# The two PSUM banks of a tile's h made neighbours, in an FFT and MoE kernel whose order a planner writes

## The chip, the cores and the metric

One core of a Trainium2 chip (trn2). The time is device microseconds of one execution, from the median of several runs. PE is TensorE (matmuls), PEld its weight loads, DVE is VectorE, ACT ScalarE, POOL GpSimd and SP SyncE, which issues nearly all DMAs.

## What is computed

Eight batches of x (3136 x 256) go through a spectral mix and then through a feed-forward layer with a softmax gate:

```python
X = np.fft.rfft(x, axis=1);  Xr, Xi = X.real, X.imag
Yr = Xr @ w_r - Xi @ w_i + b_r
Yi = Xr @ w_i + Xi @ w_r + b_i
Yr, Yi = (np.sign(Y) * np.maximum(np.abs(Y) - 0.01, 0.0) for Y in (Yr, Yi))
y = np.fft.irfft(Yr + 1j * Yi, n=3136, axis=1)      # 25088 rows of 256 in all
h = y @ w_in                                        # 256 -> 1024
solu = h * softmax(h)
ln = (solu - mean(solu)) / np.sqrt(var(solu) + 1e-6) * g_ln
out = ln @ w_out                                    # 1024 -> 256
```

## The kernel before, in words

**The work.** The front end of a batch makes the forward transform in two steps (`fwd1`, `fwd2`), the mix with the weights (`mix`), the threshold and the first inverse step (`inv1`); `inv2` writes y, split into two f16 halves, into a ring in SBUF (`ring_hi`, `ring_lo`). The back end takes 196 tiles of 128 rows from the ring. For each tile:

- `moe_head` (L1065): 12 matmuls of 512 columns write h (128 x 1024) into a tile of two PSUM banks, six matmuls into the first bank and six into the second. Then DVE takes the row maximum over both banks (the TENSOR_REDUCE `sm<-banks`), ACT makes the exponential from both banks (ACTIVATE `u<-banks,sm,hsb`), and DVE multiplies h by it (SCALAR_TENSOR_TENSOR `u<-banks,sm,u`). All three read both banks, in this order; only the third is the last reader of h.
- `moe_turn` (L1101): u is split in two f16 halves (ACT `lh`, POOL `ll`), each goes through a DMA transpose into `th` and `tl`, and ACT takes the sum of squares (`junk`).
- `moe_tail` (L1120): 16 matmuls with `th` and then 8 with `tl`, all of 256 columns, add up in one bank `po`; ACT scales it out (`o<-banks,r`).

The back end of batch b runs among the front ends of the batches b+1 and b+2, so one tile's head and tail stand between groups of the front end's matmuls. After the last front end only heads, tails and `inv2` are left.

**PSUM.** All eight banks belong to one class, `Banks` (L250). Single banks (`tile`, L264) hold the front end's results (`pf`, `pb`) and `po`; `two` (L268) is h (`ph`). `BANKS` (L54) says how many of each kind may be alive at once. `place` (L258) turns a tile's bank numbers into a slice of one allocation of 8 x 512 columns that all the tiles share:

```python
a, z = min(banks), max(banks)
return self.whole[:, a] if a == z else self.whole[:, a : z + 1 : z - a]
```

So an h in the banks 1 and 6 is a slice with a step of five banks.

**The order.** Each call is recorded as an operation of a `Plan` (L286) with a key (`KEYS`, L42, gives the keys' offsets and steps). `Plan.order` (L398) then lists the operations of all engines, as its own durations have them: at each turn it takes, among the operations of an engine that can start within `PATIENCE` ns of the first that could, the one with the lowest key. `may_start` (L418) holds an operation back until its tile has a buffer or its banks are free. Before, the free banks are a sorted list, and a tile takes the one or two that came free first, whichever they are. The instructions are then emitted in this order (`issue`, L388). Semaphores are set afterwards, by the layer under the kernel, from the slices that the instructions read and write; the planner doesn't see those. Each engine runs its list strictly in order. Nearly every instruction carries L396, the line that emits the plan, so this document goes by operands.

Of the kernel before, what the change touches and what calls it, by code (L numbers as in the profile page):

```python
# [39 lines left out]


KEYS = dict(  # L42
    front_b0=(-159.11, 1.14),
    w_in=(-164.02, -51.6, -22.9),
    w_out=(-19.52, -15.36),
    mix_w=23.18,
    front_a1=(-62.63, 6.47),
    front_a=((1.05, -7.26), (4.86, -3.51)),
    front_b=((2.24, 18.34), (-2.67, 0.08)),
    inv2=-114.18,  # L50
    turn=2.19,
    tail=4.23,
)
BANKS = dict(pf=5, ph=4, po=7, pb=7)  # L54


def fft_constants():
# [75 lines left out]
class View:  # L133
# [3 lines left out]
    def __init__(self, tile, rows, cells, dtype, path=()):  # L137
        self.tile, self.rows, self.cells, self.dtype, self.path = tile, rows, cells, dtype, path
# [111 lines left out]
class Banks:  # L250


    def __init__(self, pool, n, **most):
        self.pool, self.kinds = pool, {name: Kind(m, self) for name, m in most.items()}
        self.n, self.whole = n, None
        self.free = [(0.0, i) for i in range(n)]

    def place(self, banks):  # L258
        if self.whole is None:
            self.whole = self.pool.tile([128, self.n, 512], F32, name="banks")  # L260
        a, z = min(banks), max(banks)
        return self.whole[:, a] if a == z else self.whole[:, a : z + 1 : z - a]

    def tile(self, name):  # L264
        t = Tile(self.pool, self.kinds[name], [128, 512], F32, dict(name=name, bufs=1))
# [20 lines left out]
class Plan:  # L286
# [2 lines left out]


    ENGINES = ("gpsimd", "tensor", "vector", "scalar", "sync")
    PATIENCE = 128.0
    BACKLOG, AHEAD = 3200.0, 1500.0
    LEAVE = {2: 115.0, 4: 150.0, 8: 195.0}

# [102 lines left out]
    def order(self):  # L398
        ready = {e: [] for e in self.ENGINES}
        free = dict.fromkeys(self.ENGINES, 0.0)  # L400
        waits, bus, half, port = {}, 0.0, False, 0.0
        for op in self.ops:
            waits[op] = len(op.needs)
            for o in op.needs:
                o.next.append(op)
            if not op.needs:
                op.at = 0.0
                ready[op.engine].append(op)
        left = {t: len(t.users) for op in self.ops for t in op.tiles}

        turn, turns = {}, {}
        for t, op in sorted(((t, min(t.users, key=lambda op: op.seq)) for t in left), key=lambda x: (x[1].key, x[1].seq)):
            if t.kind.banks is None:
                turn[t] = turns.get(t.kind, 0)
                turns[t.kind] = turn[t] + 1
        done = []

        def may_start(op):  # L418
            at = max(free[op.engine], op.at, port if op.port else 0.0, bus - (self.AHEAD if op.early else self.BACKLOG) if op.moved else 0.0)
            taken = {}  # L420
            for t in op.tiles:
                if t.owner is None:
                    k = t.kind
                    n = len(k.placed) + taken.get(k, 0)
                    taken[k] = taken.get(k, 0) + 1
                    if turn.get(t, n) != n:
                        return np.inf
                    n -= k.bufs
                    if n >= 0:
                        at = max(at, k.freed[n] if n < len(k.freed) else np.inf)  # L430
                    if k.banks is not None:
                        n, spare = taken.get(k.banks, 0) + t.size, k.banks.free
                        taken[k.banks] = n
                        at = max(at, spare[n - 1][0] if n <= len(spare) else np.inf)
            return at

        while len(done) < len(self.ops):
            best = None
            for e in self.ENGINES:
                can = [(may_start(op), op) for op in ready[e]]  # L440
                if not can:
                    continue
                first = min(at for at, _ in can)
                if first == np.inf:
                    continue
                _, _, at, op = min((op.key, op.seq, at, op) for at, op in can if at <= first + self.PATIENCE)
                if best is None or at < best[0]:
                    best = at, op
            assert best is not None, "the plan is stuck"
            at, op = best  # L450
            e = op.engine
            ready[e].remove(op)
            if e == "tensor":
                if op.half != half:
                    at += 95.0 if op.half else self.LEAVE[half]
                half = op.half
            op.start = at
            op.end = free[e] = at + op.length
            if op.port:
                port = op.end  # L460
            if op.moved:
                bus = max(bus, op.end) + op.moved
                op.end = bus + 2000.0
            for t in op.tiles:
                if t.owner is None:
                    t.owner = op
                    t.kind.placed.append(t)
                    if t.kind.banks is not None:
                        t.banks = [t.kind.banks.free.pop(0)[1] for _ in range(t.size)]
                left[t] -= 1  # L470
                if not left[t]:
                    freed = max(o.end + self.SEEN[o.engine] for o in t.users)
                    insort(t.kind.freed, freed)
                    if t.kind.banks is not None:
                        for bank in t.banks:
                            insort(t.kind.banks.free, (freed, bank))
            for o in op.next:
                waits[o] -= 1
                if not waits[o]:
                    o.at = max(p.end + (0.0 if p.engine == o.engine == "tensor" else self.SEEN[p.engine]) for p in o.needs)  # L480
                    ready[o.engine].append(o)
            done.append(op)
        self.span = max(op.end for op in done)
        return sorted(done, key=lambda op: (op.start, op.seq))
# [22 lines left out]
def fft_mix_solu_kernel(ctx: ExitStack, tc, x, w_r, w_i, b_r, b_i, w_in, w_out, g_ln, fa, iaf, fa16, fb, fs, gb, gs, ia, out):  # L507
# [17 lines left out]
    sp = Pool(ctx.enter_context(tc.tile_pool(name="sp", bufs=4)), 4)  # L525
    banks = Banks(ctx.enter_context(tc.tile_pool(name="ps", bufs=1, space=PSUM)), 8, **BANKS)

# [872 lines left out]
```

## Time and profile before

| | |
|---|---|
| median of 3 runs | 1873.73 us (1868.37 to 1874.85) |
| the profiled execution, its own time | 1875.22 us |
| its span, from the first to the last instruction | 1873.4 us |
| mean granted clock of TensorE | 0.962 of 2.4 GHz |
| busy: PE, DVE, ACT, POOL | 1586.5, 1247.8, 1188.4, 1124.3 us |
| busy share of the span: PE, DVE, ACT, POOL | 85%, 67%, 63%, 60% |

How to read it: PE is the engine that is busiest in every stretch, so what counts is when PE stands still and what ends each such pause. A matmul's row lasts longer than the distance to the next one, because matmuls overlap; a group's busy time is the union of its rows.

### The profile page before, as it was taken

How to read it: one execution, taken by the hardware profiler on the slowest of the kernel's cores; microseconds unless marked ns; L12 is line 12 of the kernel's file. 1: busy time of each engine (PE TensorE's matmuls, PEld its weight loads, DVE VectorE, ACT ScalarE, POOL GpSimd, SP SyncE). 2: the span in 40 equal slices, each digit the busy share in tenths (PEclk: the TensorE clock that was granted, in tenths of full speed). 3: DMA queues.
4: the chain of work that ended last, by engine and by line, in shares of the span. 5: the costliest groups of instructions: out<-in, count | busy, mean ns of one | idle time of the engine just before them, and what ended most of it. 6: DMA issues, size and time to landing. Idle time of an engine off the chain costs nothing. (4 is left out here: it accounts for less than half of the span.)

```text
span 1873.4 us, 40978 instructions
## 1 busy us (share of the span) xinstructions
PE 1586.5 (85%) x15375; PEld 1082.4 (58%) x15375; DVE 1247.8 (67%) x2496; ACT 1188.4 (63%) x2140; POOL 1124.3 (60%) x1652
## 2 busy tenths in 40 slices
PE   7977899899888789888989899878898879977776
PEld 3444576567555566556656567555665557655554
DVE  5875688668677577656877688655777558644442
ACT  5865677767577466755767667665567657655553
POOL 1745686558665477546856578454785548745553
PEclk8988999999899899999999999999999999999999
DMA  7774756888388755767667984768748664664443
GB/s 250 238 211 100 147 100 146 188 191 195 80 196 185 173 134 131 170 154 188 151 131 169 200 192 113 165 151 180 168 94 195 145 145 101 128 129 100 93 90 80
DMA packets 531580, 285.62 MB, mean 152 GB/s; under 512 B 426500, under 2 KB 504688, under 8 KB 531380
## 3 DMA queue, kind: packets, MB, share of 16 engines
q1 hardware_dynamic: 530932, 281.39, 66.4%
q8 instruction: 120, 1.97, 0.4%
q10 hardware_dynamic: 448, 1.61, 0.3%
q14 instruction: 80, 0.66, 0.1%
HBM read 103.07 MB, written 77.07 MB: 96 GB/s over the span
## 5 line engine op out<-in xcount | busy, mean ns | idle before, releaser
L396 POOL TENSOR_TENSOR ll<-u,lh 128x1024 f16<-128x1024 f32 x196 | 423.6, 2162 | 225.4 <-ACT lh L396 223.9
L396 DVE SCALAR_TENSOR_TENSOR u<-banks,sm,u 128x1024 f32<-128x1024 f32 x196 | 251.3, 1282 | 253.4 <-PE banks L396 138.7
L396 PE MATMUL banks<-wout,th 128*128 128x256 f16 x3136 | 381.8, 276 | 19.1 <-DVE sm L396 8.0
L396 PE MATMUL banks<-win_hi,ring_hi 128*128 128x512 f16 x768 | 302.6, 394 | 81.1 <-DVE u L396 42.5
L396 ACT ACTIVATE u<-banks,sm,hsb 128x1024 f32<-128x1024 f32 x192 | 231.2, 1204 | 206.9 <-PE banks L396 123.0
L396 PEld LDWEIGHTS <-th 128*128 128x128 f16 x3136 | 308.5, 99 | 87.8 <-issue 24.7
L396 DVE TENSOR_REDUCE sm<-banks 128x1 f32<-128x1024 f32 x196 | 239.6, 1223 | 179.4 <-PE banks L396 173.0
L396 ACT CAST lh<-u 128x1024 f16<-128x1024 f32 x196 | 205.3, 1047 | 164.5 <-DVE u L396 60.1
L396 PE MATMUL banks<-win_low,ring_lo 128*128 128x512 f16 x768 | 301.6, 393 | 0.0
L396 PE MATMUL banks<-win_lo,ring_hi 128*128 128x512 f16 x768 | 301.5, 393 | 0.0
L396 PEld LDWEIGHTS <-ring_hi 128*128 128x128 f16 x1536 | 152.3, 101 | 248.3 <-issue 115.2
L396 PE MATMUL banks<-wout,tl 128*128 128x256 f16 x1568 | 205.4, 274 | 71.6 <-DVE sm L396 44.6
L396 ACT ACTIVATE junk<-u,sm 128x1024 bf16<-128x1024 f32 x196 | 225.7, 1152 | 14.8 <-DVE u L396 14.7
L396 PEld LDWEIGHTS <-tl 128*128 128x128 f16 x1568 | 152.1, 98 | 101.7 <-issue 81.6
L396 POOL TENSOR_SCALAR a<-sm 128x1 f32<-128x1 f32 x196 | 53.3, 272 | 258.8 <-ACT u L396 182.4
L396 PE MATMUL banks<-w_hi,Xh 128*128 128x256 f16 (+1 forms) x584 | 167.8, 287 | 24.7 <-DVE u L396 11.5
L396 PE MATMUL banks<-w_hi,Xl 128*128 128x256 f16 (+1 forms) x584 | 167.7, 287 | 1.1 <-DVE Xl L396 1.0
L396 PE MATMUL banks<-w_lo,Xh 128*128 128x256 f16 (+1 forms) x584 | 167.7, 287 | 0.0
L396 POOL TENSOR_TENSOR y<-yt,yc 128x512 f32<-128x512 f32 (+1 forms) x104 | 130.9, 1264 | 43.2 <-DVE yc L396 36.0
L396 PEld LDWEIGHTS <-Xh 128*128 128x128 f16 x1168 | 115.2, 100 | 62.2 <-issue 33.2
L396 ACT ACTIVATE o<-banks,r 128x256 f32<-128x256 f32 x196 | 92.3, 471 | 83.6 <-PE banks L396 38.9
L396 POOL TENSOR_TENSOR yl<-y,yh 128x512 f16<-128x512 f32 x96 | 113.5, 1186 | 50.4 <-ACT yh L396 50.2
(177 smaller groups left out, 2602.8 us busy)
## 6 DMA issues: line engine op xcount, KB each, us to landing
xt<-in_x_dram SPq DMA_DIRECT2D x104, 392.0 KB
zt<-s SPq DMA_DIRECT2D x56, 392.0 KB
s<-zout SPq DMA_DIRECT2D x42, 512.0 KB
s<-av SPq DMA_DIRECT2D x48, 392.0 KB
bin<-s SPq DMA_DIRECT2D x36, 512.0 KB
out_dram<-o SPq DMA_DIRECT2D x128, 96.0 KB
out_dram<-o SPq DMA_DIRECT2D x136, 64.0 KB
out_dram<-o SPq DMA_DIRECT2D x128, 32.0 KB
```

Source lines behind the costliest of these rows:

```text
L396: getattr(engine, name)(*args, **kw)
```

## The change

- The two banks of an h are now neighbours: `place` takes the slice `a : a + n`. A new function `pick` gives out banks: for two, the neighbouring pair that is free first; for one, a free bank that has the fewest free neighbours, so that pairs are broken up last.
- `Banks.free` holds a time for each bank instead of a sorted list. In `may_start` a pair can start when both of some neighbouring two are free; for several single banks of one operation the n-th free time counts as before.
- The numbers that set the order: all of `KEYS`, `BANKS` (pf 5 to 7, ph 4 to 5, po 7 to 4, pb 7 to 6) and `PATIENCE` (128 to 105).

The arithmetic, the tiles in SBUF and the number of instructions of each kind stay as they are.

```diff
--- before.py
+++ after.py
@@ -40,18 +40,18 @@
 
 
 KEYS = dict(
-    front_b0=(-159.11, 1.14),
-    w_in=(-164.02, -51.6, -22.9),
-    w_out=(-19.52, -15.36),
-    mix_w=23.18,
-    front_a1=(-62.63, 6.47),
-    front_a=((1.05, -7.26), (4.86, -3.51)),
-    front_b=((2.24, 18.34), (-2.67, 0.08)),
-    inv2=-114.18,
-    turn=2.19,
-    tail=4.23,
+    front_b0=(-160.94, 0.2),
+    w_in=(-167.38, -90.32, -6.8),
+    w_out=(-63.87, -1.11),
+    mix_w=254.87,
+    front_a1=(-97.59, 12.01),
+    front_a=((1.73, -0.57), (1.25, 3.43)),
+    front_b=((4.04, 44.05), (-4.76, -2.95)),
+    inv2=-122.76,
+    turn=1.47,
+    tail=4.26,
 )
-BANKS = dict(pf=5, ph=4, po=7, pb=7)
+BANKS = dict(pf=7, ph=5, po=4, pb=6)
 
 
 def fft_constants():
@@ -253,13 +253,13 @@
     def __init__(self, pool, n, **most):
         self.pool, self.kinds = pool, {name: Kind(m, self) for name, m in most.items()}
         self.n, self.whole = n, None
-        self.free = [(0.0, i) for i in range(n)]
+        self.free = [0.0] * n
 
     def place(self, banks):
         if self.whole is None:
             self.whole = self.pool.tile([128, self.n, 512], F32, name="banks")
-        a, z = min(banks), max(banks)
-        return self.whole[:, a] if a == z else self.whole[:, a : z + 1 : z - a]
+        a, n = banks[0], len(banks)
+        return self.whole[:, a] if n == 1 else self.whole[:, a : a + n]
 
     def tile(self, name):
         t = Tile(self.pool, self.kinds[name], [128, 512], F32, dict(name=name, bufs=1))
@@ -289,7 +289,7 @@
 
 
     ENGINES = ("gpsimd", "tensor", "vector", "scalar", "sync")
-    PATIENCE = 128.0
+    PATIENCE = 105.0
     BACKLOG, AHEAD = 3200.0, 1500.0
     LEAVE = {2: 115.0, 4: 150.0, 8: 195.0}
 
@@ -429,10 +429,21 @@
                     if n >= 0:
                         at = max(at, k.freed[n] if n < len(k.freed) else np.inf)
                     if k.banks is not None:
-                        n, spare = taken.get(k.banks, 0) + t.size, k.banks.free
+                        n, spare = taken.get(k.banks, 0) + 1, k.banks.free
                         taken[k.banks] = n
-                        at = max(at, spare[n - 1][0] if n <= len(spare) else np.inf)
+                        at = max(at, sorted(spare)[n - 1] if t.size == 1 else min(map(max, spare, spare[1:])))
             return at
+
+        def pick(free, size, at):
+            if size == 2:
+                a = min(range(len(free) - 1), key=lambda i: (max(free[i], free[i + 1]), i))
+                banks = [a, a + 1]
+            else:
+                beside = lambda i: sum(0 <= j < len(free) and free[j] <= at for j in (i - 1, i + 1))
+                banks = [min(range(len(free)), key=lambda i: (free[i] > at, beside(i), free[i], i))]
+            for i in banks:
+                free[i] = np.inf
+            return banks
 
         while len(done) < len(self.ops):
             best = None
@@ -466,14 +477,14 @@
                     t.owner = op
                     t.kind.placed.append(t)
                     if t.kind.banks is not None:
-                        t.banks = [t.kind.banks.free.pop(0)[1] for _ in range(t.size)]
+                        t.banks = pick(t.kind.banks.free, t.size, at)
                 left[t] -= 1
                 if not left[t]:
                     freed = max(o.end + self.SEEN[o.engine] for o in t.users)
                     insort(t.kind.freed, freed)
                     if t.kind.banks is not None:
                         for bank in t.banks:
-                            insort(t.kind.banks.free, (freed, bank))
+                            t.kind.banks.free[bank] = freed
             for o in op.next:
                 waits[o] -= 1
                 if not waits[o]:
```

What this does to the order, at two places. In these rows `[waits ...]` names the semaphores that an instruction waits for: `DVE_49`, `Activation_49`, `PE_49` and `Pool_49` count the instructions of an engine, `DMAHW...` the DMAs.

PE, in the last batch, where a tail goes from `th` to `tl` in one and the same bank `po`. Before:

```order
L396 LDWEIGHTS th
L396 MATMUL banks<-wout,th 128x256
L396 LDWEIGHTS tl [waits DMAHW2_49]
L396 MATMUL banks<-wout,tl 128x256 [waits DVE_49]
L396 LDWEIGHTS tl
L396 MATMUL banks<-wout,tl 128x256
```

and now:

```order
L396 LDWEIGHTS th
L396 MATMUL banks<-wout,th 128x256
L396 LDWEIGHTS tl [waits DMAHW6_49]
L396 MATMUL banks<-wout,tl 128x256
L396 LDWEIGHTS tl
```

The `tl` group still waits for its transpose (DMAHW), but no longer for DVE. Of the 196 `tl` groups 52 waited for DVE or ACT before, and none does now.

DVE, in the last batch, one h from one tile's multiplication to the next one's. Before:

```order
L396 SCALAR_TENSOR_TENSOR u,sm<-banks,sm,u 128x1024 [waits PE_49,DVE_49,Activation_49,Pool_49]
L396 TENSOR_REDUCE sm<-banks 128x1 [waits PE_49,Activation_49]
L396 TENSOR_SCALAR sm<-sm,hsb 128x1 [waits DVE_49]
L396 TENSOR_SCALAR sm<-sm 128x1 [waits DVE_49]
L396 TENSOR_SCALAR sm<-sm,hsb 128x1 [waits DVE_49]
L396 SCALAR_TENSOR_TENSOR u,sm<-banks,sm,u 128x1024 [waits PE_49,DVE_49,Activation_49,Pool_49]
```

and now:

```order
L396 SCALAR_TENSOR_TENSOR u,sm<-banks,sm,u 128x1024 [waits DVE_49,Activation_49,Pool_49]
L396 TENSOR_REDUCE sm<-banks 128x1 [waits PE_49]
L396 TENSOR_SCALAR sm<-sm,hsb 128x1 [waits DVE_49]
L396 TENSOR_SCALAR sm<-sm 128x1 [waits DVE_49]
L396 TENSOR_SCALAR sm<-sm,hsb 128x1 [waits DVE_49]
L396 SCALAR_TENSOR_TENSOR u,sm<-banks,sm,u 128x1024 [waits DVE_49,Activation_49,Pool_49]
```

The same instructions stand in the same order; the reduction no longer waits for ACT, and the multiplication no longer for PE (it reads an h for which the reduction had already waited).

## Rows read from the trace of the kernel before

**Rows 1.** The page's head and its first part: the span, and of each engine busy time, share of the span and instructions.

```profile
span 1873.4 us, 40978 instructions
...
PE 1586.5 (85%) x15375; PEld 1082.4 (58%) x15375; DVE 1247.8 (67%) x2496; ACT 1188.4 (63%) x2140; POOL 1124.3 (60%) x1652
```

**Rows 2.** The waits of PE alone, longest in total first, over the whole span: who waited <- for whom: us in total, times, longest.

```profile
PE banks L396 <- DVE u L396: 89.9, 77, 3.3
PE banks L396 <- DVE sm L396: 82.6, 70, 2.1
PE banks L396 <- ACT u L396: 74.8, 66, 2.6
PE banks L396 <- DMA zt<-s2f: 9.0, 1, 9.0
PE banks L396 <- ACT bin L396: 5.8, 1, 5.8
PE banks L396 <- DMA out_dram<-o: 4.2, 3, 1.4
```

**Rows 3.** Groups of PE instructions by operands and shape, whole span: busy us, mean ns of one | idle us of PE just before them, and what ended most of it.

```profile
L396 PE MATMUL banks<-wout,th 128*128 128x256 f16 x3136 | 381.8, 276 | 19.1 <-DVE sm L396 8.0 <-DVE u L396 6.7 <-ACT u L396 2.8
L396 PE MATMUL banks<-win_hi,ring_hi 128*128 128x512 f16 x768 | 302.6, 394 | 81.1 <-DVE u L396 42.5 <-ACT u L396 33.3 <-DVE sm L396 4.4
...
L396 PE MATMUL banks<-wout,tl 128*128 128x256 f16 x1568 | 205.4, 274 | 71.6 <-DVE sm L396 44.6 <-ACT u L396 16.6 <-DVE u L396 7.6
...
L396 PE MATMUL banks<-w_hi,Xh 128*128 128x256 f16 x536 | 148.6, 277 | 23.3 <-DVE u L396 11.5 <-DVE sm L396 8.1 <-ACT u L396 3.3
L396 PE MATMUL banks<-ia_s,zt 98*128 98x98 f16 x1344 | 73.4, 209 | 20.0 <-DVE sm L396 11.7 <-DVE u L396 4.4 <-ACT u L396 3.8
```

**Rows 4.** Timeline of PE in the last batch, 1800 to 1812 us: start us, us, what, in brackets the idle time before it and what ended it.

```profile
1800.29 0.38 PE L396 MATMUL banks<-win_lo,ring_hi 128*128 128x512 f16 x1
1800.51 0.38 PE L396 MATMUL banks<-win_low,ring_lo 128*128 128x512 f16 x1
1800.72 1.91 PE L396 MATMUL banks<-wout,th 128*128 128x256 f16 x16
1804.02 1.03 PE L396 MATMUL banks<-wout,tl 128*128 128x256 f16 x8 [1.38 <-DVE sm L396]
1806.44 0.38 PE L396 MATMUL banks<-win_hi,ring_hi 128*128 128x512 f16 x1 [1.39 <-ACT u L396]
1806.65 0.38 PE L396 MATMUL banks<-win_lo,ring_hi 128*128 128x512 f16 x1
...
1808.81 0.38 PE L396 MATMUL banks<-win_low,ring_lo 128*128 128x512 f16 x1
1809.45 1.91 PE L396 MATMUL banks<-wout,th 128*128 128x256 f16 x16 [0.26 <-DVE u L396]
```

**Rows 5.** Timeline of DVE in the same stretch.

```profile
1802.74 1.23 DVE L396 TENSOR_REDUCE sm<-banks 128x1 f32<-128x1024 f32 x1 [1.75 <-PE banks L396]
1804.00 0.21 DVE L396 TENSOR_SCALAR sm<-sm,hsb 128x1 f32<-128x1 f32 x1
1804.25 0.15 DVE L396 TENSOR_SCALAR sm<-sm 128x1 uint32<-128x1 uint32 x1
1804.44 0.21 DVE L396 TENSOR_SCALAR sm<-sm,hsb 128x1 uint32<-128x1 uint32 x1
1808.11 1.28 DVE L396 SCALAR_TENSOR_TENSOR u<-banks,sm,u 128x1024 f32<-128x1024 f32 x1 [3.45 <-PE banks L396]
...
1811.39 1.22 DVE L396 TENSOR_REDUCE sm<-banks 128x1 f32<-128x1024 f32 x1 [2.00 <-PE banks L396]
```

**Rows 6.** Timeline of ACT in the same stretch.

```profile
1801.02 0.47 ACT L396 ACTIVATE o<-banks,r 128x256 f32<-128x256 f32 x1 [3.81 <-DVE u L396]
...
1805.09 1.21 ACT L396 ACTIVATE u<-banks,sm,hsb 128x1024 f32<-128x1024 f32 x1 [1.52 <-PE banks L396]
1806.19 0.19 ACT L396 ACTIVATION_READ_ACCUMULATOR u<-banks,sm,hsb 128x1 f32 x1
1806.29 0.46 ACT L396 ACTIVATE o<-banks,r 128x256 f32<-128x256 f32 x1
```

**Rows 7.** The waits of all engines, the three rows in which DVE and ACT wait for PE.

```profile
DVE sm L396 <- PE banks L396: 173.0, 113, 7.0
DVE u L396 <- PE banks L396: 138.7, 62, 5.4
ACT u L396 <- PE banks L396: 127.3, 68, 6.2
```

**Rows 8.** Busy time of each engine by stretch (us, then PE, PEld, DVE, ACT, POOL with the count of instructions), granted clock of TensorE as a share of 2.4 GHz, mean busy share of the DMA engines, GB/s.

```profile
0.00:150.00 150.00, 121.27 (x1016) 66.17 (x1017) 111.29 (x239) 98.56 (x191) 67.92 (x74) 0.88 0.73 223
150.00:300.00 150.00, 125.69 (x1299) 90.34 (x1298) 102.67 (x199) 93.77 (x166) 102.67 (x141) 0.95 0.59 117
300.00:650.00 350.00, 309.35 (x2961) 212.61 (x2960) 248.38 (x489) 234.64 (x424) 217.01 (x325) 0.97 0.77 172
650.00:1000.00 350.00, 302.11 (x3148) 209.95 (x3147) 247.16 (x498) 226.50 (x403) 222.59 (x321) 0.97 0.66 152
1000.00:1350.00 350.00, 300.32 (x3009) 209.25 (x3013) 241.91 (x474) 223.98 (x406) 210.47 (x313) 0.97 0.75 167
1350.00:1700.00 350.00, 301.17 (x3075) 210.24 (x3060) 230.99 (x465) 227.77 (x412) 223.55 (x340) 0.98 0.63 134
1700.00:1874.00 174.00, 126.60 (x897) 83.83 (x894) 65.44 (x135) 83.22 (x142) 80.10 (x142) 0.97 0.45 89
```

**Rows 9.** The same for three single stretches of 100 us.

```profile
400.00:500.00 100.00, 91.86 (x1156) 68.42 (x1154) 80.77 (x158) 65.98 (x127) 74.61 (x98) 0.97 0.75 168
1000.00:1100.00 100.00, 87.35 (x764) 60.21 (x761) 68.70 (x130) 64.13 (x120) 54.99 (x90) 0.98 0.85 187
1600.00:1700.00 100.00, 83.44 (x741) 57.90 (x740) 55.12 (x115) 61.14 (x111) 63.19 (x103) 1.00 0.61 129
```

## The prediction

> **What bounds the kernel now.** I read the page's head first, then the waits of PE, then the groups of its instructions, and last a timeline to see what one such wait is made of. PE is busy for 1586.5 of 1873.4 us, DVE, ACT and POOL for 60 to 67% [rows 1]; PE is also the busiest engine of every stretch [rows 8]. So the kernel is as long as PE's work plus PE's pauses, 1873.4 - 1586.5 = 286.9 us. Three reasons make up 89.9 + 82.6 + 74.8 = 247.3 us of the pauses, in 77 + 70 + 66 = 213 waits: DVE's `u` (the multiplication), DVE's `sm` (the maximum) and ACT's `u` (the exponential). Waits for DMAs are small: 9.0 and 4.2 us in rows 2.
>
> These three are the readers of h, and this looks like a lack of banks: PE waits until h is read. It isn't that. The maximum and the exponential are never the last readers of an h; the multiplication is. No bank comes free when they end, yet they end 82.6 + 74.8 = 157.4 us of the pauses. Clearer still is the `tl` group of a tail. It adds to the bank that the `th` group opened just before, so it needs no new bank at all, but 44.6 + 16.6 + 7.6 = 68.8 us pass before `tl` groups for these three reasons [rows 3].
>
> One instance shows the mechanism. The head ends with the matmul that starts at 1800.51 and lasts 0.38; `th` runs until 1802.63; then PE stands for 1.38 us until the maximum ends at 1803.97, runs `tl`, and stands for another 1.39 us until the exponential has ended [rows 4 to 6]. In the built program this h lies in the banks 1 and 6, the `po` of the tail in bank 5, and the next head begins in bank 2. The banks 5 and 2 lie between 1 and 6. The semaphores treat a slice with a step as all that lies between its ends. It goes both ways: the maximum could start when the head is done, at 1800.89, but starts at 1802.74, after `th` [rows 5]. PE, DVE and ACT go in lockstep, each waiting for a bank that the other doesn't touch.
>
> I followed the semaphore counts in both built programs. Of PE's waits for another compute engine, 283 are for an instruction that shares neither a bank nor a tile with the waiting one; in the changed program 32. With neighbours nothing lies between.
>
> The Trainium skill (PSUM — Partial Sum Buffer, the section on bank collisions) asks for a guard by bank and quadrant; rows 4 to 6 show a guard that is far wider than that, and what it costs.
>
> **The change part by part.**
>
> *Waits that go.* The maximum and the exponential: 157.4 us, all of it. The multiplication's 89.9 us are mixed, since it does free banks. 89.9 - 42.5 = 47.4 us of it stand before groups other than the head [rows 2, 3]; I count them in, as the built program has nearly all such waits on a foreign bank. Before the head's matmuls, 35 of 63 such waits are on a foreign bank, so 42.5 x 35/63 = 24. Together 157.4 + 47.4 + 24 = 229 us. Bounds: 205 (nothing of the 42.5) and 247 (all of it).
>
> *Pipeline.* A matmul row lasts 0.38 us and the next one starts 0.21 us later (1806.44, 1806.65) [rows 4]. Before each pause PE counts some 0.165 us as busy that would lie over the next matmul. With 229/247 of 213 waits, 197 x 0.165 = 32 us. Bounds 0 and 35.
>
> *Clock.* The clock is either 1.2 or 2.4 GHz; between 300 and 1700 us its mean is 0.97 to 0.98 of full [rows 8], which is worth about 0.0275 x 1400 = 39 us, and it is 1.00 in a stretch whose PE is busy for only 83% [rows 9]. So pauses alone don't fix it. Between 0 and 39 I take 15, under the middle, because of that stretch.
>
> The Trainium skill (TensorE: Matmul & The Clock Gate, Part 1) says the lower level is what an idle engine falls back to, and by that the shorter pauses would give back most of the 39 us; the sum would then be some 20 us lower.
>
> *Waits that come.* Only neighbours will do now, so a pair can be missing where two free banks would have been enough. What counts is how much PE work lies between the end of a head and the next writer of its banks. In rows 4 and 5 the banks are held from 1800.89 to 1808.11 + 1.28 = 1809.39, or 8.5 us, but with lockstep in it. Without it the parts are 1.23 + 0.21 + 0.15 + 0.21 (DVE), 1.21 (ACT) and 1.28 (DVE), 4.3 us, some 5 to 6 with the gaps between. I added up PE's work in the order of each program, at the distances that rows 4 show. In the changed program 77 of 388 banks of h are written again after less than 8.5 us, with 70 us missing in all (before: 42 of 389, with 35 us); after less than 6 us only one, with 0.6 us missing. So between 1 and 70 us come as real waits. I take 35, the middle, and 10 for the other kinds of bank, together 45.
>
> *The moved order.* Every engine has the same instructions as before, and SP's one queue of DMAs is rearranged with the rest. I cost this at nothing: DVE, the next busiest, has 248.4 of 350 us to do in its fullest long stretch [rows 8], and takes up a permutation as long as PE leads. If that cover goes, the second rival tells the price. The start stays: until the first heads PE waits for the DMA `zt` (9.0) and for ACT's `bin` (5.8) [rows 2], and the first instructions hardly move.
>
> *Sum.* The profiled execution's own time is 1875.2 us, 0.1% over the median of 1873.7. 1875.2 - 229 - 32 - 15 + 45 = 1644; I give 1645 us.
>
> **The rivals.**
>
> *1. Pairs run short, and it gets slower.* Single banks stand so that no two neighbours are free when a head is due; PE then waits for the head each time. All the savings together come to 276 us, so it decides from 276/196 = 1.4 us of waiting per tile. At 2 us it would be 1875 - 276 + 392 = 1991 us. For it: eight banks and pairs only, and `po` falls from 7 to 4. Against it: PE's work between two uses is almost never under 6 us, and a single bank goes first where it breaks up no pair.
>
> The Trainium skill (Perfetto Trace Analysis, Optimization Strategy) says that bubbles that repeat on the engine that should be saturated can mean that there isn't enough PSUM for the next tile. By that reading the pauses are a lack of banks and a stricter choice of banks makes them longer: this rival. The trace doesn't agree: `tl` groups, which need no bank, wait for 68.8 us [rows 3].
>
> *2. Another engine takes over for a part.* With the pauses gone, the middle is 13% shorter, and DVE, 81% busy in its fullest 100 us, or the DMA engines, 0.85 in theirs [rows 9], would come near 95% there. The pauses in the two stretches with a DMA share over 0.7 are 350 - 309.4 + 350 - 300.3 = 90 us [rows 8]. If half to all of it comes back as waits for late data, 1690 to 1735 us; with the 70 us of bank waits too, 1760. For it: those peaks. Against it: hardly any of PE's pauses ends with a DMA now.
>
> *3. The change doesn't do what it says.* The semaphores are still drawn wider than the banks, or all 247 us are replaced by equal waits for the readers of h: about 1870 us. Against it: in the changed order no `tl` group waits for DVE or ACT, and 52 did.
>
> **How the numbers follow.** Forecast (1600 to 1690 us): 0.62. Rival 2: 0.27. Rival 3: 0.03. Rival 1: 0.04. Even better than 1600, with the upper bounds of what goes (247 + 35 + 39, so 1555 with 1 us of new waits): 0.04. The range takes in the forecast and most of rival 2: 1600 to 1740. A measurement of this kernel tells some 0.5% from no change. Faster by more than that are the forecast, rival 2 and the better case, 0.93; within it rival 3, 0.03; slower rival 1, 0.04.
>
> **What the profile after would show.** Right: PE's waits for DVE `sm` and ACT `u` fall from 157 to under 10 us; `tl` groups have next to no pause; PE's busy share rises from 85% to about 94%, at some 1550 us; what is left of the pauses before the head ends with DVE `u`, at up to 70 us; DVE's wait for PE before the maximum and ACT's before the exponential [rows 7] are of heads alone, and the hold of h in the last batch falls from 8.5 towards 6 us. The prediction would be wrong if pauses before heads grow past 100 us with DVE `u` as their end (rival 1), if DMA shares of 0.95 or waits of PE for `th`, `tl`, `zt` or POOL's results show up (rival 2), or if `sm` still ends pauses of PE (rival 3).

## The result, and the profile after

| | before | after |
|---|---|---|
| median | 1874.29 us (4 runs, 1868.37 to 1875.59) | 1537.62 us (4 runs, 1534.77 to 1538.47) |
| the profiled execution: own time, span | 1875.22, 1873.4 us | 1534.77, 1532.7 us |
| mean granted clock | 0.962 | 0.990 |

The ratio is 0.8206, 95% interval [0.8186, 0.8227]: 337 us less, where the forecast was 1645 us in a range from 1600 to 1740. It also lies under the 1555 us of the better case, to which the prediction gave a chance of 0.04. The direction and the mechanism held; the size didn't.

The head of the page after, answering to [rows 1]:

```profile
span 1532.7 us, 40928 instructions
...
PE 1506.8 (98%) x15375; PEld 1064.5 (69%) x15375; DVE 1223.0 (80%) x2496; ACT 1182.7 (77%) x2140; POOL 1139.1 (74%) x1652
```

PE pauses for 1532.7 - 1506.8 = 25.9 us instead of 286.9, and its own busy time is 79.7 us shorter. The waits of PE [rows 2] are now (who waited <- for whom: us in total, times, longest):

```profile
PE banks L396 <- ACT bin L396: 5.7, 1, 5.7
PE banks L396 <- DMA zt<-s2f: 3.5, 1, 3.5
PE banks L396 <- ACT Xh L396: 1.8, 1, 1.8
...
PE banks L396 <- ACT u L396: 0.9, 1, 0.9
```

The 247.3 us for the three readers of h are down to one wait of 0.9 us for the exponential; the maximum and the multiplication don't appear at all. The groups [rows 3] show the same from the other side (busy us, mean ns of one | idle us before):

```profile
L396 PE MATMUL banks<-wout,th 128*128 128x256 f16 x3136 | 374.5, 273 | 0.2 <-DVE zout L396 0.2
L396 PE MATMUL banks<-win_hi,ring_hi 128*128 128x512 f16 x768 | 292.0, 380 | 0.0
...
L396 PE MATMUL banks<-wout,tl 128*128 128x256 f16 x1568 | 203.4, 273 | 0.0
L396 PE MATMUL banks<-w_hi,Xh 128*128 128x256 f16 x536 | 146.2, 273 | 0.0
...
L396 PE MATMUL banks<-ia_s,zt 98*128 98x98 f16 x1344 | 68.5, 206 | 0.3 <-DMA zt<-s 0.3
```

The `tl` groups, which waited for 71.6 us, have no pause, and the head's first matmuls none either, where 81.1 us stood. PE's timeline in the last batch, where rows 4 had two pauses per tile:

```profile
1455.40 0.38 PE L396 MATMUL banks<-win_lo,ring_hi 128*128 128x512 f16 x1
1455.62 0.38 PE L396 MATMUL banks<-win_low,ring_lo 128*128 128x512 f16 x1
1455.83 1.91 PE L396 MATMUL banks<-wout,th 128*128 128x256 f16 x16
1457.58 1.04 PE L396 MATMUL banks<-wout,tl 128*128 128x256 f16 x8
1458.45 0.38 PE L396 MATMUL banks<-win_hi,ring_hi 128*128 128x512 f16 x1
```

and DVE's in the same stretch [rows 5]:

```profile
1456.03 1.23 DVE L396 TENSOR_REDUCE sm<-banks 128x1 f32<-128x1024 f32 x1 [0.95 <-PE banks L396]
1457.29 0.21 DVE L396 TENSOR_SCALAR sm<-sm,hsb 128x1 f32<-128x1 f32 x1
1457.54 0.15 DVE L396 TENSOR_SCALAR sm<-sm 128x1 uint32<-128x1 uint32 x1
1457.73 0.21 DVE L396 TENSOR_SCALAR sm<-sm,hsb 128x1 uint32<-128x1 uint32 x1
1458.98 1.28 DVE L396 SCALAR_TENSOR_TENSOR u<-banks,sm,u 128x1024 f32<-128x1024 f32 x1 [1.04 <-ACT u L396]
```

The head ends at 1456.00, and the maximum starts at 1456.03, not after the tail. The banks of this tile are held until 1458.98 + 1.28 = 1460.26, for 4.3 us where the tile in rows 4 and 5 had 8.5. PE runs head, tail and the next head without a gap. By stretch [rows 8] (us, then PE, PEld, DVE, ACT, POOL, granted clock, DMA share, GB/s):

```profile
0.00:150.00 150.00, 128.99 (x1104) 69.66 (x1105) 116.01 (x252) 103.23 (x200) 71.25 (x73) 0.90 0.75 227
150.00:300.00 150.00, 149.69 (x1592) 110.05 (x1591) 126.60 (x253) 119.47 (x214) 127.30 (x181) 1.00 0.78 164
300.00:650.00 350.00, 349.53 (x3722) 251.30 (x3721) 304.43 (x611) 282.73 (x507) 268.76 (x387) 1.00 0.93 206
650.00:1000.00 350.00, 350.00 (x3779) 253.25 (x3778) 291.87 (x597) 277.27 (x502) 274.72 (x394) 1.00 0.90 194
1000.00:1350.00 350.00, 350.00 (x3711) 254.32 (x3709) 278.18 (x564) 270.21 (x494) 272.37 (x401) 1.00 0.82 174
1350.00:1533.00 183.00, 178.56 (x1479) 125.91 (x1477) 105.93 (x223) 129.82 (x227) 124.68 (x221) 1.00 0.73 143
```

From 300 to 1350 us PE is busy for 1049.5 of 1050 us at the full clock, with DVE at up to 304.4 of 350 and the DMA engines at up to 0.93. DVE still waits for PE before the maximum [rows 7], but in the built program for heads alone, and the multiplication's wait for the exponential, whose result it needs, is now the longer one:

```profile
DVE u L396 <- ACT u L396: 80.4, 98, 1.9
DVE sm L396 <- PE banks L396: 78.9, 96, 2.7
```

### The profile page after: what moved, and what is told of

It is laid out like the page before. It is cut to its first block, busy times and chain, and to the rows that moved or that the text cites. A ratio compares the mean times of both kernels' runs of the same rounds, so it can differ in the third digit from the quotient of the medians.

```text
span 1532.7 us, 40928 instructions
## 1 busy us (share of the span) xinstructions
PE 1506.8 (98%) x15375; PEld 1064.5 (69%) x15375; DVE 1223.0 (80%) x2496; ACT 1182.7 (77%) x2140; POOL 1139.1 (74%) x1652
## 4 chain that ended last, share of the span: by engine, by line
PE 90%; DMA 3%; ACT 3%; POOL 2%; DVE 1%; issue 1%; SPq 0%; ACTq 0%; DVEq 0%; POOLq 0%
PE banks L396 90%; DMA xt<-in_x_dram 1%; DMA zt<-s2f 0%; DMA u<-in_x_dram 0%; POOL y L396 0%; DMA xt<-s1f 0%; POOL ll L396 0%; DMA zt<-in_w_r_dram 0%; ACT Xh L396 0%; DVE yt L396 0%; POOL r L396 0%; DMA zt<-s 0%; ACT zout L396 0%; DVE Xl L396 0%; SPq L396 0%
## 5 line engine op out<-in xcount | busy, mean ns | idle before, releaser
L396 PE MATMUL banks<-wout,th 128*128 128x256 f16 x3136 | 374.5, 273 | 0.2 <-DVE zout L396 0.2
L396 PEld LDWEIGHTS <-th 128*128 128x128 f16 x3136 | 304.5, 98 | 61.0 <-issue 1.9
L396 PE MATMUL banks<-win_hi,ring_hi 128*128 128x512 f16 x768 | 292.0, 380 | 0.0
L396 PE MATMUL banks<-win_lo,ring_hi 128*128 128x512 f16 x768 | 291.8, 380 | 0.0
L396 PE MATMUL banks<-win_low,ring_lo 128*128 128x512 f16 x768 | 291.7, 380 | 0.0
L396 PEld LDWEIGHTS <-ring_hi 128*128 128x128 f16 x1536 | 148.7, 98 | 141.8 <-issue 2.3
L396 POOL TENSOR_TENSOR y<-yt,yc 128x512 f32<-128x512 f32 (+1 forms) x104 | 142.1, 1370 | 48.1 <-DVE yc L396 33.3
L396 POOL TENSOR_SCALAR a<-a,hsb 128x1 f32<-128x1 f32 x384 | 128.3, 334 | 14.7
L396 PEld LDWEIGHTS <-ring_lo 128*128 128x128 f16 x768 | 75.2, 98 | 91.1 <-issue 0.6
L396 POOL TENSOR_TENSOR yl<-y,yh 128x512 f16<-128x512 f32 x96 | 116.9, 1220 | 16.6 <-ACT yh L396 15.8
```

Of the source, the lines that this page charges most:

```text
L396: getattr(engine, name)(*args, **kw)
```

## The experiments

The theory (A): nearly all of the gain is the semaphore waits that were drawn over the banks lying between the two of an h. Rivals: the new numbers and the order they make (B); neighbours cost real waits that the numbers make up for (C).

**Placing alone.** The changed code with the old numbers:

```diff
-    front_b0=(-160.94, 0.2),
+    front_b0=(-159.11, 1.14),
...
-BANKS = dict(pf=7, ph=5, po=4, pb=6)
+BANKS = dict(pf=5, ph=4, po=7, pb=7)
...
-    PATIENCE = 105.0
+    PATIENCE = 128.0
```

> The neighbouring placement of the changed kernel with the numbers (KEYS, BANKS, PATIENCE) of the kernel before. Theory A (the gain is the semaphore waits on banks that lie between the two of an h): no such wait is left in this program, so 1540 to 1600 us, most of the 337 us, with PE's idle time under 80 us. Rival B (the gain is the new order that the new numbers make): close to the kernel before, 1800 to 1875 us. Rival C (neighbours cost real waits for pairs, and the numbers were needed to make up for them): 1620 to 1720 us, with PE pauses before heads that end with DVE u.

Measured: 1542.86 us, 0.8238 [0.8205, 0.8270] of before. PE's waits, longest first:

```profile
PE banks L396 <- ACT th L396: 9.7, 1, 9.7
PE banks L396 <- ACT bin L396: 5.8, 1, 5.8
PE banks L396 <- DVE u L396: 2.1, 3, 1.2
```

The multiplication is left with 2.1 us in three waits. The placing alone gives all that can be told from the whole change: the two intervals overlap. B and C fall. The plan was made anew for this run, so the order isn't that of the kernel before either; the run with the same order, below, takes that doubt away.

**Numbers alone.** The converse: the code of before with the new `KEYS`, `BANKS` and `PATIENCE`.

> The kernel before with the new numbers alone: any two banks, the slice with a step. 294 waits of PE are for a reader of an h that shares no bank with the waiting matmul (kernel before: 256, changed kernel: 0). Theory A: 1850 to 1950 us, no faster than before. Rival B: 1540 to 1650 us. Rival C: between, around 1800 us.

Measured: 1946.45 us, 1.0398 [1.0350, 1.0447] of before, so slower. The three readers of h end more of PE's pauses than before, 302 us instead of 247:

```profile
PE banks L396 <- ACT u L396: 102.8, 84, 2.8
PE banks L396 <- DVE u L396: 101.0, 78, 3.0
PE banks L396 <- DVE sm L396: 98.4, 79, 2.8
```

**The same order, banks apart.** The sharpest test leaves the changed kernel's order on every engine as it is and renumbers the banks where the slice is made:

```diff
-        a, n = banks[0], len(banks)
-        return self.whole[:, a] if n == 1 else self.whole[:, a : a + n]
+        banks = [(0, 4, 1, 5, 2, 6, 3, 7)[i] for i in banks]
+        a, z = min(banks), max(banks)
+        return self.whole[:, a] if a == z else self.whole[:, a : z + 1 : z - a]
```

> The changed kernel, its plan and the order on every engine unchanged, but when the slices are made the eight banks are renumbered 0,4,1,5,2,6,3,7, so that no h lies in neighbours and each slice has a step again. Nothing else changes; 368 waits of PE are now for a reader of an h on a foreign bank. Theory A: 1875 to 2020 us (368/256 of the loss of before gives 2020), with PE pauses that end with DVE sm and ACT u. Rivals B and C: the order decides and is the same, so 1535 to 1560 us.

Measured: 1997.43 us, 1.0667 [1.0624, 1.0710] of before. In the built programs not a working instruction differs in kind or place on any engine; only the bank numbers do, and the semaphores that follow from them. 460 us are back, more than the change gave, as this program has 368 waits for a foreign bank where the kernel before had 256. PE's waits (the emitting line is now L397):

```profile
PE banks L397 <- DVE u L397: 130.2, 115, 3.0
PE banks L397 <- ACT u L397: 124.4, 103, 2.9
PE banks L397 <- DVE sm L397: 102.0, 96, 2.7
```

**In doses.** The same edit with other renumberings: `(0, 1, 2, 4, 3, 5, 6, 7)` puts two of the seven pairs apart, `(0, 2, 1, 3, 4, 6, 5, 7)` four, `(0, 2, 4, 1, 3, 6, 5, 7)` six (the last run's name says five).

> As the run above, but only the banks 3 and 4 change places: of the seven pairs of neighbours two then have one foreign bank between them. 49 waits of PE are for a reader of an h on a foreign bank. Theory A with a loss in proportion to the waits: 337 x 49/256 = 64 us more, so 1600 us; 1550 to 1580 if the queues behind take up a part. Rivals B and C: no change, 1537 us.

> The changed kernel with the banks renumbered 0,2,1,3,4,6,5,7 when the slices are made: four of the seven pairs have one foreign bank between them; plan and order unchanged. 125 waits of PE are for a reader of an h on a foreign bank (0 in the changed kernel, 49 and 368 in the two such runs before, which cost 53 and 460 us, 1.1 and 1.25 us for each). Theory A with a price per wait: 1537 + 125 x 1.1 to 1.25, so 1670 to 1695 us. If the queues behind take up scattered waits: under 1640. On the clock: if the lower level comes with these pauses, the share of time lost to it (1 - granted clock, times the span) lies between the 21 us of the run with two pairs apart and the 56 us of the one with all apart.

> As the run above with the renumbering 0,2,4,1,3,6,5,7, so that the slices of six of the seven pairs have foreign banks between them. 201 waits of PE on a foreign bank. Theory A with 1.1 to 1.25 us for each: 1760 to 1790 us. Time lost to the lower clock: above the run with 125 waits and not over 60 us; if the clock doesn't follow these pauses, it stays at the changed kernel's 15 us.

| renumbering | PE waits on a foreign bank | median | more than 1537.6 us | for each wait | time lost to the lower clock |
|---|---|---|---|---|---|
| none (changed kernel) | 0 | 1537.62 | 0 | | 1532.7 x 0.010 = 15 us |
| two pairs apart | 49 | 1590.86 | 53 | 1.09 us | 1590.7 x 0.013 = 21 us |
| four | 125 | 1674.68 | 137 | 1.10 us | 1674.5 x 0.015 = 25 us |
| six | 201 | 1742.90 | 205 | 1.02 us | 1738.6 x 0.017 = 30 us |
| all | 368 | 1997.43 | 460 | 1.25 us | 1993.5 x 0.028 = 56 us |

The second column counts waits for a reader of an h that shares no bank with the waiting matmul, in the built programs; the kernel before has 256 of them. The time follows this count at 1.0 to 1.25 us for each; the run with six pairs apart came out 17 us under its expectation. That is a price for the renumbering and not for PE's waits alone: the readers of h wait for PE's work on foreign banks too (54 such waits with two pairs apart, 315 with all, none in the changed kernel), and the lower clock is in it. The time lost to the lower clock, an estimate as span x (1 - mean granted clock), rises with the waits. The smallest dose, PE's waits:

```profile
PE banks L397 <- DVE u L397: 16.3, 15, 2.1
PE banks L397 <- DVE sm L397: 13.4, 11, 1.3
PE banks L397 <- ACT bin L397: 5.7, 1, 5.7
PE banks L397 <- ACT u L397: 5.5, 7, 1.2
```

**The rule for single banks.** Is it needed that a single bank breaks up no pair? In `pick`:

```diff
-                banks = [min(range(len(free)), key=lambda i: (free[i] > at, beside(i), free[i], i))]
+                banks = [min(range(len(free)), key=lambda i: (free[i], i))]
```

> The changed kernel, but a single bank is the one that came free first, without the rule that it should break up no pair (the plan is made anew). Theory D (h is held for about 6 us now, median of the changed kernel's trace, and real waits for banks come only where less PE work than that lies before the next writer): 5 such places in this program's order with 4.6 us missing, so 1535 to 1555 us. Rival E (the rule for single banks is what keeps pairs available, without it heads wait): 1580 to 1700 us with PE pauses before heads that end with DVE u.

Measured: 1548.91 us, 0.8276 [0.8247, 0.8305]. That lies clear of the changed kernel's interval, by about 11 us, and in the range of D: pairs are found without the rule too. Only 3.7 us of PE's pauses in this run end with the multiplication, and its plan was made anew, so it isn't shown that the 11 us are lost on pairs.

**Fewer banks.** How far is the changed kernel from a real lack of pairs? `Banks` is given 7 or 6 banks of the 8 (the allocation keeps its size):

```diff
-    banks = Banks(ctx.enter_context(tc.tile_pool(name="ps", bufs=1, space=PSUM)), 8, **BANKS)
+    banks = Banks(ctx.enter_context(tc.tile_pool(name="ps", bufs=1, space=PSUM)), 7, **BANKS)
```

> The changed kernel on seven of the eight banks (the plan is made anew). Theory D, with a hold of 6 us: 23 places with 15.6 us missing, so about 1545 to 1575 us. With the hold of 8.5 us that the prediction used: 99 places, 144 us missing, 1610 to 1680 us. If the changed kernel had no room left in PSUM (rival E): over 1650 us.

> The changed kernel on six of the eight banks (the plan is made anew). Theory D, with a hold of 6 us: 31 places with 10 us missing (at 7 us 98 places and 76 us), so 1560 to 1640 us. With a hold of 8.5 us: 212 places, 314 us missing, over 1750 us. If no pauses of PE appear that end with a reader of h, the scarcity of pairs isn't a cost of any size in this kernel.

Measured: 1571.65 us with seven (0.8399 [0.8365, 0.8433]) and 1619.28 with six (0.8646 [0.8605, 0.8687]). Both lie within D. With a quarter of PSUM gone the kernel is still 254 us faster than before, and what it loses isn't lost on pairs. Two groups of PE with six banks:

```profile
L396 PE MATMUL banks<-wout,th 128*128 128x256 f16 x3136 | 382.0, 276 | 42.7 <-ACT Xh L396 18.5 <-DVE zout L396 9.0 <-DVE Xl L396 6.6
L396 PE MATMUL banks<-win_hi,ring_hi 128*128 128x512 f16 x768 | 292.8, 381 | 3.1 <-DVE u L396 3.1
```

Heads pause for 3.1 us; the 42.7 us stand before tails, and end with readers of the front end's single banks (`Xh`, `zout`, `Xl`). So where D put the price, on the banks of h, it was wrong, though the time fell into its range.

**What lies behind PE.** The changed kernel without the tail's matmuls with `tl` (the low half of u isn't multiplied):

```diff
-        for part, halves in ((th, 2), (tl, 1)):
+        for part, halves in ((th, 2),):
...
-                        nc.tensor.matmul(po[:, :D], part[:, f], wout[:, f, j], start=n == 0, stop=n == 3 * NF - 1)
+                        nc.tensor.matmul(po[:, :D], part[:, f], wout[:, f, j], start=n == 0, stop=n == 2 * NF - 1)
```

> The changed kernel without the tail's 8 matmuls with tl (the low half of u is made and transposed but not multiplied): 1568 matmuls less, at 0.109 us from one to the next 171 us of PE work. If PE's work is all that bounds the changed kernel: 1537 - 171 = 1366 us, up to 1390. If DVE (80% busy) or the DMA engines (0.93 of a stretch) are close behind (rival 2 of the prediction): 1430 to 1500 us, with PE pauses that end with a DMA or with results of the front end.

Measured: 1496.29 us, 0.8002 [0.7966, 0.8038]. Of 171 us of PE work, an estimate from 1568 matmuls at 0.109 us, only 41 come off. The head of its page and PE's waits:

```profile
span 1502.9 us, 37734 instructions
...
PE 1382.2 (92%) x13807; PEld 929.7 (62%) x13807; DVE 1218.0 (81%) x2496; ACT 1168.8 (78%) x2140; POOL 1136.6 (76%) x1652
```

```profile
PE banks L396 <- DMA zt<-s: 19.1, 6, 5.3
PE banks L396 <- DVE u L396: 16.8, 18, 2.2
PE banks L396 <- DMA th<-lh: 10.9, 6, 2.7
PE banks L396 <- ACT yh L396: 8.2, 2, 4.8
```

PE pauses for 1502.9 - 1382.2 = 120.7 us instead of 25.9, spread over many reasons: loads of `zt` and transposes into `th` that come late, the multiplication, the front end's splits. PE's busy time falls by 124.6 us and not by 171, and the clock has a part in that: it is 0.959 here, and by the estimate used above 1502.9 x 0.041 = 62 us are lost to the lower level instead of 15. So PE's work does bound the changed kernel, but a field of others stands some 40 us behind it, and the pauses that they make cost clock as well. No single one is named by this run, and its plan was made anew.

## Why the prediction was wrong

*Right.* What bounded the kernel, which of its pauses were waits for a bank that the other doesn't touch, and that neighbours would take them away: all shown by the run with the same order and other bank numbers. Set beside the built program, the trace before agrees pause by pause: 240 us of pauses that end with a reader of h stand before matmuls that share no bank with that h, and 2 us before matmuls that do. The profile after has the `tl` groups without a pause, the lockstep gone, the hold of h shorter and the three reasons under 10 us, as forecast. The new numbers cost nothing: with and without them the time is the same within what can be told.

*Wrong: the sizes of four terms, all to the same side.* The largest is the waits that come, put at 45 us, of which none came; the clock, put at 15 us, gave back 45. The spans differ by 340.7 us; 261.0 of it are pauses and 79.7 are PE's busy time.

| term of the sum | forecast | measured | from |
|---|---|---|---|
| waits for h's readers that go | -229 | -246 | 247.3 [rows 2], 0.9 left |
| other pauses of PE | 0 | -15 | 286.9 - 247.3 = 39.6 before, 25.9 - 0.9 = 25.0 after |
| matmuls' ends before pauses | -32 | -35 | 213 pauses x 0.165 us, worked out, not measured apart |
| clock | -15 | -45 | the rest of the 79.7 us of busy time; point 2 has it from the clock itself |
| waits that come | +45 | 0 | none of any size in the waits of PE after |

1. *The waits that come* was the largest miss. The count of PE's work between two uses of a bank was sound; the hold that I set against it wasn't. I used the middle between 8.5 us, which has the lockstep in it, and 5 to 6 us, although I had just worked out that the lockstep would go. With the short hold the count itself said 0.6 us missing. Set beside the program's order, the trace after has a median of 6.0 us from the last matmul into a bank of h to the end of the multiplication, before 8.8 us (392 banks each). The same comparison bears the count out: 75 of 388 banks of h are written again less than 8.5 us after their last matmul, where I had counted 77. But these were held for 5.6 us in the median and for 7.7 at most, and PE paused for none of them. Banks that are held for over 8.5 us exist after the change too, 18% of them; no matmul wants them early. So one hold for all banks was wrong as well as too long. The runs with seven and six banks show how much room there was.

2. *The clock.* I took 15 of at most 39 us, since one stretch had the full clock with PE busy for 83% [rows 9]. After, it is 1.00 in every stretch from 150 us on. The time lost to the lower level falls from 1873.4 x 0.038 = 71 to 15 us. That share of the span includes PE's pauses, in which a lower clock costs nothing. Half of the time that PE was busy at the lower level, 1.2 of 2.4 GHz, falls from 57 to 12 us: 45 us, as the table has it. Of these, 35 lie between 300 and 1700 us, near the 39 of the prediction; the other 10 lie in the first 300 us and at the end, which that bound left out. The rule of the Trainium skill that I had weighed against the row (TensorE: Matmul & The Clock Gate, Part 1) agrees with the trace here, and my row was one stretch of 100 us. The doses show the loss rising with the pauses, 15 to 56 us, but not in proportion to them: the kernel before, with 256 such waits in another order, lost 71.

3. *The multiplication before heads.* I split its 42.5 us by counts, 24 to 18, and held the 18 for real waits for a bank. None is left. Set beside the built program, the trace before has 42.3 us of pauses in 32 heads that waited for the multiplication on a foreign bank, and 1.3 us in 3 heads on a bank of their own (all 196 heads; the row has 192). The count took every semaphore alike; those that named the head's own bank were hardly ever the late ones.

The sum with the measured terms is 1875.2 - 246 - 15 - 35 - 45 = 1534, the profiled time. It has to come out so, since the clock's term is a rest; what speaks for it is that the clock's own record gives the same 45. With the short hold (0.6 us of new waits, and none for other kinds of bank) and all 39 us of the clock my own terms would have given some 1575 us.

*The rivals.* The first (pairs run short, slower) didn't happen and is far off: two banks less cost 82 us. The reading of the bubbles as a lack of PSUM, from the Trainium skill (Perfetto Trace Analysis, Optimization Strategy), doesn't fit this trace: 256 waits for foreign banks were the cause, and six banks with exact waits beat eight with wide ones. The second (others take over) is true of the field behind PE, as the run without `tl` shows, but not of this change: DMA shares of 0.90 to 0.93 over 700 us and DVE at 87% left PE without a pause. I had priced it by shares of busy time alone, and left out the first 150 us, whose DMA share of 0.73 is over 0.7 as well [rows 8]. The third (the semaphores stay wide) fell with the result: 0.9 of 247.3 us are left.

## What to carry to other kernels

When an engine waits for an instruction, ask whether the two share the bank or the tile: a wait that ends with a reader that is never the last, or that stands before a group whose bank is already open, is a semaphore drawn too wide, and a slice with a step is where to look. To price what replaces such waits, use durations as they will be without them, not as the lockstep made them. To prove it, keep the order and change only the addresses.

## What the runs showed of the hardware that I had not expected

PE ran for 1050 us with 0.5 us of pauses [the stretches after], at the full clock throughout, beside DMA engines at up to 0.93 and DVE at up to 87%; I had expected something to come late at 95%. One thing got slower: POOL's subtraction `y` took 1309 ns before and 1402 after, with the same operands. Busier engines alone don't explain it. With the placing alone, a kernel as dense as the changed one, it took 1292 ns; with the same order and the banks apart, the longest run of all, 1392. From the top: before, after, placing alone, same order with the banks apart.

```profile
L396 POOL TENSOR_TENSOR y<-yt,yc 128x512 f32<-128x512 f32 x96 | 125.1, 1309 | 39.5 <-DVE yc L396 33.4 <-ACT yt L396 3.7 <-DVE sm L396 1.2
L396 POOL TENSOR_TENSOR y<-yt,yc 128x512 f32<-128x512 f32 x96 | 134.2, 1402 | 44.2 <-DVE yc L396 33.3 <-DVE sm L396 5.7 <-ACT yt L396 3.6
L396 POOL TENSOR_TENSOR y<-yt,yc 128x512 f32<-128x512 f32 x96 | 123.8, 1292 | 28.0 <-DVE yc L396 23.2 <-ACT yt L396 4.1
L397 POOL TENSOR_TENSOR y<-yt,yc 128x512 f32<-128x512 f32 x96 | 133.3, 1392 | 94.2 <-DVE yc L397 66.9 <-DVE sm L397 20.6 <-ACT yt L397 4.2
```

All runs with the changed kernel's order, and the one with the numbers alone, lie between 1388 and 1407 ns. So the duration goes with the order that the new numbers make, as far as these runs tell. What in that order slows it wasn't tried, and no pause of PE after names `y`.
